# A fused attention and expert kernel: key weights folded like the query weights, in 16 tiles turned by DMA, and a new order of the first loads

## The chip, the core and the metric

The kernel runs on one core of a Trainium2 chip. A core has five engines with a queue each: PE (matrix products; its weight loads are listed as PEld), DVE and ACT (elementwise work and copies), POOL (elementwise work) and SP (here it only issues transfers, as ACT does for some). The transfers of all queues run on 16 DMA engines. The metric is the time of one execution in microseconds (us); lower is better.

## The reference, cut to what matters

There are 2048 tokens of width 1024, 32 heads of width 32, all in bf16.

```python
qkv = x @ wqkv                                     # [2048, 3 x 1024]: q, k, v
pq = q . w_phi ; pk = k . w_phi                    # per head, w_phi is 32 x 32
phi_q = concat(softmax(pq), softmax(-pq))          # 64 features a head; phi_k likewise
kv = phi_k^T v ; z = sum(phi_k)
a = ((phi_q kv) / (phi_q z + 1e-6)) @ wo           # linear attention
i = argmax(x @ w_r)                                # one token is chosen
y = (silu(x_i @ w_gate) * (x_i @ w_up)) @ w_down   # an expert of width 3584 for that token
b = x, with y * sigmoid(r_i) added to row i
g = sigmoid(x . gate_w)
out = g * a + (1 - g) * b
```

## The kernel before, in words

Tokens are worked on in 16 tiles of 128 (index `t`); the inner dimension 1024 is cut in 8 blocks of 128 (`kb`). Since `x @ w @ w_phi` is `x @ (w w_phi)`, the kernel first folds `w_phi` into the key and query weights: `wkf` and `wqf`, 128 x 8 x 1024 each. All products then need the transposed tokens `xT`.

Its stages follow each other on PE:

- *Start.* `spin` runs matmuls on constants while the first loads are under way. Token tiles 0 and 1 are transposed on PE (`xT_tile`, line 285), all others by DMA (`xT_dma`, line 299). `v_first` (line 595) computes the values of tiles 0 and 1, block by block as `wv_sb` arrives in eight loads (line 277). Two small rows (`rows`) are turned by one matmul (`rows_in`) into two more columns of `wv_sb`; they give the router and gate products.
- *Value stage.* `k_v(t, c)` computes the values of one tile in three column parts (`c` = 0, 1, 2, of 256, 384 and 386 columns), eight matmuls each, and ACT copies them out. Between these parts the weights are folded. The transposed weight blocks come by DMA (`wT_load`, line 304) into the buffers `shv`, eight blocks for keys, then eight for queries in the same places.
- *Key stage.* `feats(u, wkf, False)` for 32 units of half a tile (eight matmuls of 512 columns and the softmax), then `k_kv` (`kvps`).
- *Query stage.* `feats(u, wqf, True)`, a DMA turn, `q_num` (`num`) and the output product `q_wo` (`po`), interleaved by due times in a running count of PE time.
- *Expert.* Its three rounds and a half of gate and up weights (`gu_load`, `ffn_gu`, `facc`) run at units 9, 16 and 23 of the key stage, the down product in the query stage. The weight chunks (`wch`) go through buffers that other things have left: W and V (one tile), A (a ring of three), D (the two `shv`), X and Y (the place of `wv_sb`).

The folds of keys and queries differ. For a key block, `fold` multiplies by a block-diagonal 128 x 128 matrix `BDm` with four copies of `w_phi` a block: eight matmuls of 128 columns, two casts on DVE, and the result stands in `wkf` as it is used. For the queries, `qfold` works in 32 x 32 tiles of PE, 16 at a time:

```python
nc.tensor.matmul(banks[r][32*c:32*c+32, :]..., lhsT=BDm[32*r:32*r+32, j, 32*r:32*r+32],
                 rhs=shv[half][32*r:32*r+32, :, j*P:(j+1)*P], ..., tile_position=(32*r, 32*c))
```

Four such packs (table `PACKS`) give the transposed folded weight `wfT`, in two buffers of the ring that A uses too; eight DMA transposes (`qfold_turn`, line 334) turn it into `wqf` during the key stage, after units 4 and 7. `q_heads` (line 161) reads the turned weight in its head order.

Where nothing pins an instruction, the scheduler of the language may move it on its queue; `tc.keep_in_program_order` pins it. Each transfer of SP and ACT has one of eight completion semaphores in turn, so it waits for the one issued eight before it. `gate_load` (line 459) lets POOL write one element of the first three weight chunks after the last `wT_load` has landed, which keeps the expert's loads behind the transposes. `route` finds the chosen token after the last values; `route_row` loads its row.

Of the kernel before, what the change touches and what calls it, by code (L numbers as in the profile page):

```python
# [38 lines left out]
FOLDS = [0] * 5 + [1] * 8 + [0] * 3  # L39
PACKS = {(13, 2): (0, 0), (14, 1): (1, 0), (15, 0): (0, 1), (15, 2): (1, 1)}  # L40
# [3 lines left out]
def general_path(tc, A_wqkv, A_w_phi, A_wo, x2, out2, gate, omg, y2, idx_pool, xT, wqf, ident, BDm):  # L44
# [27 lines left out]
    oo = gp.tile([P, D], BF, name="g_oo")  # L72

    nc.sync.dma_start(out=wv[:], in_=w_v[:, :, 2 * D:3 * D])
# [95 lines left out]
def kernel(  # L170
# [8 lines left out]
    wphi_v = A_w_phi.rearrange("(j hq) d f -> hq d j f", hq=4)  # L179
# [21 lines left out]
    def spin(n):  # L201
        for _ in range(n):
            nc.tensor.matmul(small_ps[:, 0:512], lhsT=ones, rhs=ones4, start=True, stop=True)
# [5 lines left out]
    BDm = const.tile([P, KB, P], BF, name="BDm")  # L209
    ones4 = nc.const_aps.tensor_like(1.0, BDm[:, 0:4, :].rearrange("p j f -> p (j f)"))  # L210
    rows = const.tile([P, P], BF, name="rows")
    nc.vector.memset(rows[:], 0.0)
    nc.vector.memset(BDm[:], 0.0)
    xT = big.tile([P, KB, S], BF, name="xT")
    wqf = big.tile([P, KB, D], BF, name="wqf")
# [50 lines left out]
    def xload(t, eng):  # L266
        xt_ = shv[1][:, 2 + t, :]
        eng.dma_start(out=xt_, in_=x2[t * P:(t + 1) * P, :])
        xtiles[t] = xt_
# [3 lines left out]
    xload(1, nc.scalar)  # L273
    nc.scalar.dma_start(out=rows[0:KB, :], in_=B_w_r.rearrange("(kb p) -> kb p", p=P))
    nc.scalar.dma_start(out=rows[KB:2 * KB, :], in_=gate_w.rearrange("(kb p) -> kb p", p=P))
    for kb in range(KB):
        nc.sync.dma_start(out=wv_sb[:, kb, 0:D], in_=w_v[:, kb, 2 * D:3 * D])  # L277

    def rows_in():
        rows_ps = m2_ps[:, 0:2 * KB]  # L280
        nc.tensor.matmul(rows_ps, lhsT=rows[:], rhs=ident[:, 0:2 * KB], start=True, stop=True)
        nc.vector.tensor_copy(out=wv_sb[:, :, D:VW].rearrange("p k c -> p c k"),
                              in_=rows_ps.rearrange("p (c k) -> p c k", c=2))

    def xT_tile(t):
        xt_ = xtiles.pop(t)
        for q4 in range(4):
            pool, tag = ((psB, "pB"), (psA, "pA"))[q4 // 2]
            pT = pool.tile([P, 2, P], F32, name="pT", tag=tag)
            for k2 in range(2):  # L290
                kb = q4 * 2 + k2
                nc.tensor.matmul(pT[:, k2, :], lhsT=xt_[:, kb * P:(kb + 1) * P], rhs=ident[:], start=True, stop=True)
            (nc.vector.tensor_copy if q4 % 2 == 0 else nc.scalar.copy)(
                out=xT[:, q4 * 2:q4 * 2 + 2, t * P:(t + 1) * P], in_=pT[:])
            if (t, q4) == (1, 3):
                nc.vector.tensor_copy(out=m2_ps[0:1, 0:1], in_=xT[0:1, 5, P:P + 1])
                rows_in()

    def xT_dma(t):
        nc.sync.dma_start_transpose(out=xT[:, :, t * P:(t + 1) * P], in_=x2[t * P:(t + 1) * P, :])  # L300
# [3 lines left out]
    def wT_load(which, kb):  # L304
        n = kb
        wT[which, kb] = shv[n // 4][:, n % 4, :].rearrange("p (k f) -> p k f", f=P)
        nc.sync.dma_start_transpose(out=wT[which, kb],
                                    in_=A_wqkv[kb * P:(kb + 1) * P, (1 - which) * D:(2 - which) * D])

    def fold(which, wf, kb):  # L310
        for jh in range(2):
            pW = psB.tile([P, 4, P], F32, name="pW", tag="pB")
            for j4 in range(4):
                j = jh * 4 + j4
                nc.tensor.matmul(pW[:, j4, :], lhsT=wT[which, kb][:, j, :], rhs=BDm[:, j, :],  # L315
                                 start=True, stop=True)
            nc.vector.tensor_copy(out=wf[:, kb, jh * 512:(jh + 1) * 512].rearrange("p (j f) -> p j f", f=P), in_=pW[:])  # L317

    def qfold(a, half):
        if (a, half) == (0, 0):  # L320
            moe["wfT"] = [ring.tile([P, 4, D], BF, name="wfT", tag="wch") for _ in range(2)]
        pB = psB.tile([P, 512], F32, name="pW", tag="pB")
        banks = [b[:] for b in vbank + [pB]]
        for r in range(4):
            for c in range(4):
                j = 4 * a + c
                nc.tensor.matmul(banks[r][32 * c:32 * c + 32, :].rearrange("p (k d) -> p k d", d=P),  # L327
                                 lhsT=BDm[32 * r:32 * r + 32, j, 32 * r:32 * r + 32],
# [467 lines left out]
    while i < 2 * NU or n_next < NU or wos:  # L796
# [50 lines left out]
        if i == 0:  # L847
            route_row()
# [89 lines left out]
```

## Time and profile before

| | us |
|---|---|
| median of three runs (lowest, highest) | 267.17 (266.39, 267.59) |
| the profiled execution | 266.67 |
| its span | 265.0 |
| PE busy | 258.0 |
| DVE busy | 181.9 |
| POOL busy | 126.3 |
| ACT busy | 124.8 |

The span is measured on the engines and lies 1.67 us under the time of the same execution. Busy times of matmuls overlap, so what a matmul costs is read from the starts of those that follow each other, not from its duration. The rows below come from the page of this execution and from queries of its trace.

### The profile page before, as it was taken

To read this page: it belongs to the slowest core of one execution; us is meant where nothing else is said; L and a number is where in the kernel's file an instruction comes from. 1 tells how busy PE (TensorE), PEld (TensorE's weight loads), DVE (VectorE), ACT (ScalarE), POOL (GpSimd) and SP (SyncE) were. 2 spreads that over 40 slices of the span, in tenths; PEclk is the share of its full clock that TensorE was granted. 3 is DMA by queue.
4 is the path that set the end of the run, shared out by engine and by line. 5 is a ranking of instruction groups with operands and counts; after the bars stand their busy time and mean duration, and the time that the engine had idled before them with its cause. 6 is when DMAs were issued, how large, how long until landed. Compare 5 with 4: busy or idle time off the path is not lost.

```text
span 265.0 us, 5298 instructions
## 1 busy us (share of the span) xinstructions
PE 258.0 (97%) x1976; PEld 138.8 (52%) x1999; DVE 181.9 (69%) x319; ACT 124.8 (47%) x257; POOL 126.3 (48%) x86
## 2 busy tenths in 40 slices
PE   7999999999999999999999999999999999999994
PEld 2666767765444554545555455455444544544542
DVE  4010323315789685998788789799898797898872
ACT  3143333337776454554556676447362553435210
POOL 6000000000084999579989887655536555455001
PEclk9999999999999999999999999999999999999998
DMA  7989999938999869999958999998999899979742
GB/s 228 255 143 200 187 170 189 151 79 310 405 359 201 189 102 391 401 356 362 383 200 322 208 172 182 181 215 200 242 210 197 155 195 158 227 150 179 182 119 68
DMA packets 110970, 58.45 MB, mean 221 GB/s; under 512 B 93580, under 2 KB 98780, under 8 KB 110940
## 3 DMA queue, kind: packets, MB, share of 16 engines
q1 hardware_dynamic: 108140, 53.39, 84.1%
q10 hardware_dynamic: 2768, 4.67, 7.2%
q8 instruction: 17, 0.28, 0.5%
q14 instruction: 13, 0.11, 0.1%
q0 software_dynamic: 32, 0.00, 0.0%
HBM read 31.27 MB, written 4.20 MB: 134 GB/s over the span
## 4 chain that ended last, share of the span: by engine, by line
PE 95%; DMA 2%; issue 1%; SPq 0%; DVE 0%; ACT 0%
PE pq L622 21%; PE pk L622 21%; PE po L726 21%; PE pv L583 19%; PE kvps L653 3%; PE num L687 3%; PE facc L519 2%; DMA wv_sb<-in_A_wqkv_dram 2%; PE pW L315 1%; PE pv L609 1%; PE small_ps L537 1%; PE vbank L609 1%; PE vbank L327 1%; DVE oo L730 0%; SPq L277 0%
## 5 line engine op out<-in xcount | busy, mean ns | idle before, releaser
L640 POOL TENSOR_TENSOR phi<-e,rq 128x1024 bf16<-128x1024 bf16 x63 | 119.6, 1912 | 65.3 <-DVE rq L636 38.8
L632 DVE TENSOR_REDUCE ssum<-e 128x32 f32<-128x1024 bf16 x64 | 77.4, 1211 | 16.2 <-ACT e L628 16.1
L622 PEld LDWEIGHTS <-xT 128*128 128x128 bf16 x512 | 47.4, 98 | 52.3 <-issue 1.1
L622 PE MATMUL pq<-wqf,xT 128*128 128x512 bf16 x256 | 60.3, 379 | 0.0
L622 PE MATMUL pk<-wkf,xT 128*128 128x512 bf16 x245 | 59.2, 379 | 0.6
L726 PE MATMUL po<-wo_sb,oT 128*128 128x512 bf16 (+2 forms) x252 | 58.4, 372 | 0.6
L583 PE MATMUL pv<-wv_sb,xT 128*128 128x256 bf16 (+2 forms) x336 | 50.8, 307 | 0.0
L583 PEld LDWEIGHTS <-xT 128*128 128x128 bf16 x336 | 31.9, 97 | 15.4 <-issue 0.5
L591 ACT CAST v_all<-pv 128x384 bf16<-128x384 f32 (+1 forms) x45 | 20.1, 448 | 36.8 <-PE pv L583 31.1
L726 PEld LDWEIGHTS <-oT 128*128 128x128 bf16 x264 | 23.9, 98 | 23.3
L627 ACT ACTIVATE e<-pq 128x512 bf16<-128x512 f32 x32 | 18.9, 592 | 36.2 <-PE pq L622 34.5
L317 DVE CAST wkf<-pW 128x512 bf16<-128x512 f32 x16 | 10.3, 686 | 32.1 <-PE pW L315 32.1
L627 ACT ACTIVATE e<-pk 128x512 bf16<-128x512 f32 x32 | 19.1, 597 | 27.9 <-PE pk L622 23.4
L730 DVE SCALAR_TENSOR_TENSOR oo<-po,gate,xg 128x512 bf16<-128x512 f32 (+2 forms) x33 | 24.0, 727 | 4.4 <-PE po L726 4.3
L461 POOL COPY wch<-shv 1x1 bf16<-1x1 bf16 x3 | 0.4, 177 | 54.0 <-DMA shv<-in_A_wqkv_dram 54.0
L636 DVE RECIPROCAL rq<-ssum 128x32 f32<-128x32 f32 x64 | 21.8, 342 | 1.3
L692 DVE TENSOR_TENSOR o_sb<-num,rden 128x512 bf16<-128x512 f32 x32 | 21.6, 674 | 0.8
L628 ACT ACTIVATE e<-pk 128x512 bf16<-128x512 f32 x32 | 18.9, 591 | 0.0
L628 ACT ACTIVATE e<-pq 128x512 bf16<-128x512 f32 x32 | 18.9, 590 | 0.0
L711 ACT ACTIVATE xg<-xin,omg 128x1024 f32<-128x1024 bf16 x16 | 18.4, 1149 | 0.4
L687 PEld LDWEIGHTS <-phT 128*128 128x128 bf16 x256 | 12.4, 98 | 7.8 <-issue 0.3
L653 PEld LDWEIGHTS <-phi 128*128 128x128 bf16 x256 | 11.8, 98 | 7.6 <-issue 0.8
(129 smaller groups left out, 149.9 us busy)
## 6 DMA issues: line engine op xcount, KB each, us to landing
wch<-in_B_w_down_dram SPq DMA_DIRECT2D x7, 1024.0 KB
wch<-in_B_w_up_dram SPq DMA_DIRECT2D x6, 1024.0 KB
wch<-in_B_w_gate_dram SPq DMA_DIRECT2D x4, 1024.0 KB
xin<-in_A_x_dram ACTq DMA_DIRECT2D x16, 256.0 KB
out_dram<-oo SPq DMA_DIRECT2D x30, 128.0 KB
wch<-in_B_w_gate_dram SPq DMA_DIRECT2D x4, 768.0 KB
wv_sb<-in_A_wqkv_dram SPq DMA_DIRECT2D x8, 256.0 KB
wo_sb<-in_A_wo_dram SPq DMA_DIRECT2D x1, 2048.0 KB
```

Of the source, the lines that this page charges most:

```text
L583: nc.tensor.matmul(pv[:, 0:hi - lo], lhsT=xT[:, kb, t * P:(t + 1) * P], rhs=wv_sb[:, kb, lo:hi], start=(kb == 0), stop=(kb == KB - 1))
L591: copy(out=v_all[:, t, h0:h1, 0:DH], in_=pv[:, 0:(h1 - h0) * DH].rearrange("p (h d) -> p h d", d=DH))
L622: nc.tensor.matmul(pk[:].rearrange("p (c r) f -> p c r f", r=4) if is_q else pkf, lhsT=xT[:, kb, t * P:(t + 1) * P], rhs=q_heads(wf, kb, h ...
L627: nc.scalar.activation(out=e[:, :, 0, :], in_=pk[:], func=ACTF.Exp)
L628: nc.scalar.activation(out=e[:, :, 1, :], in_=pk[:], func=ACTF.Exp, scale=-1.0)
L632: nc.vector.tensor_reduce(out=ssum[:], in_=e2, axis=AX.X, op=ALU.add)
L636: nc.vector.reciprocal(out=rs, in_=ssum[:])
L640: eng.tensor_tensor(out=phi[:].rearrange("p h s f -> p (h s) f"), in0=e2, in1=_bc(rs, [P, HH * 2, DH]), op=ALU.mult)
L687: nc.tensor.matmul(num[:, pl * 66:pl * 66 + 66], lhsT=phT[:, pl, :], rhs=KV[hf][:, pl, :], start=True, stop=True)
L692: nc.vector.tensor_tensor(out=st["o"][:, hf * HH:(hf + 1) * HH, :].rearrange("p (r h) d -> p r h d", h=2), in0=nv[:, :, :, 0:DH], in1=rden ...
L726: nc.tensor.matmul(po[:, 0:w], lhsT=st["oT"][:, kb, :], rhs=moe["wo"][:, kb, sl], start=(kb == 0), stop=(kb == KB - 1))
L730: nc.vector.scalar_tensor_tensor(out=o_out[:, 0:w], in0=po[:, 0:w], scalar=gate[:, t:t + 1], in1=st["xg"][:, sl], op0=ALU.mult, op1=ALU.add)
```

## The change

Three things are changed.

- The key weights are folded as the query weights are: four more packs of 16 matmuls, after parts (5, 1), (6, 0), (8, 2) and (9, 1) of the value stage, in place of eight times eight matmuls with `BDm`. The results stand in the place of `wqf`, which is free until the query turns, and eight DMA transposes turn them into `wkf`. `BDm` is now built on the rarely taken general path alone; `w_phi` comes in one load (`wph`) where four filled `BDm`. The key features read `wkf` through `q_heads`.
- Token tile 1 is loaded by SP behind tile 0, where ACT loaded it. Both tiles are transposed on PE before the first value product, one constant matmul fewer stands ahead, and `v_first` takes its parts in another order.
- The order of SP's queue is pinned: key turns 0 to 3, the last four query blocks, key turns 4 to 7, and behind them the first expert chunks. The gate on POOL is gone. The first two chunks of the third round go ahead of the second four query turns. The last value parts of tiles 14 and 15 come in another order (`ORDER`), and `route` is called when three of them are still to come, where before one was.

```diff
-FOLDS = [0] * 5 + [1] * 8 + [0] * 3
-PACKS = {(13, 2): (0, 0), (14, 1): (1, 0), (15, 0): (0, 1), (15, 2): (1, 1)}
+PACKS = {(5, 1): (0, 0, 0), (6, 0): (0, 1, 0), (8, 2): (0, 0, 1), (9, 1): (0, 1, 1),
+         (13, 2): (1, 0, 0), (14, 1): (1, 1, 0), (15, 0): (1, 0, 1), (15, 2): (1, 1, 1)}
+ORDER = {14: ((14, 2), (15, 2), (14, 0)), 15: ((14, 1), (15, 0), (15, 1))}
...
 xload(0, nc.sync)
-xload(1, nc.scalar)
...
 for kb in range(KB):
-    nc.sync.dma_start(out=wv_sb[:, kb, 0:D], in_=w_v[:, kb, 2 * D:3 * D])
+    if kb == 0:
+        xload(1, nc.sync)
+    pin(nc.sync.dma_start(out=wv_sb[:, kb, 0:D], in_=w_v[:, kb, 2 * D:3 * D]))
...
-    def fold(which, wf, kb):
-        for jh in range(2):
-            pW = psB.tile([P, 4, P], F32, name="pW", tag="pB")
-            for j4 in range(4):
-                j = jh * 4 + j4
-                nc.tensor.matmul(pW[:, j4, :], lhsT=wT[which, kb][:, j, :], rhs=BDm[:, j, :],
-                                 start=True, stop=True)
-            nc.vector.tensor_copy(out=wf[:, kb, jh * 512:(jh + 1) * 512]..., in_=pW[:])
-    def qfold(a, half):
+    def fold(which, a, half):
         if (a, half) == (0, 0):
-            moe["wfT"] = [ring.tile([P, 4, D], BF, name="wfT", tag="wch") for _ in range(2)]
+            if which == 0:
+                wfT[0] = [wqf[:, 4 * n:4 * n + 4, :] for n in range(2)]
+            else:
+                wfT[1] = [ring.tile([P, 4, D], BF, name="wfT", tag="wch")[:] for _ in range(2)]
...
-                                 lhsT=BDm[32 * r:32 * r + 32, j, 32 * r:32 * r + 32],
+                                 lhsT=wph[32 * r:32 * r + 32, j, :],
...
-    def qfold_turn(ar):
-        nc.sync.dma_start_transpose(out=wqf[:, :, ar * P:(ar + 1) * P], in_=moe["wfT"][ar // 4][:, ar % 4, :])
+    def fold_turn(which, ar):
+        return nc.sync.dma_start_transpose(out=(wkf, wqf)[which][:, :, ar * P:(ar + 1) * P],
+                                           in_=wfT[which][ar // 4][:, ar % 4, :])
...
     def gu_load(r, kp, where):
         w = wbuf(where)
-        gate_load(w[0:1, 0:1])
...
     def v_first():
+        spin(6)
+        xT_tile(0)
+        xT_tile(1)
...
+        part(0, 0, 0)
+        part(0, 0, 1)
+        rows_in()
+        for t, kb, c in ((1, 0, 0), (0, 1, 0), (0, 1, 1), (1, 0, 1), (1, 1, 0), (1, 1, 1),
+                         (0, 0, 2), (1, 0, 2), (0, 1, 2), (1, 1, 2)):
+            part(t, kb, c)
+        for kb in range(2, KB - 1):
+            for t in range(2):
+                for c in range(3):
+                    part(t, kb, c)
...
-                             rhs=q_heads(wf, kb, hf) if is_q else wf[:, kb, hf * 512:(hf + 1) * 512],
+                             rhs=q_heads(wf, kb, hf),
...
+            if (t, n) in PACKS:
+                fold(*PACKS[t, n])
+            if (t, n) == (8, 2):
+                for ar in range(4):
+                    pin(fold_turn(0, ar))
+            if (t, n) == (9, 1):
+                for kb in range(4, KB):
+                    wT_load(1, kb)
+                for ar in range(4, 8):
+                    pin(fold_turn(0, ar))
+                moe["gu", 0] = [gu_load(0, k, b) for k, b in enumerate("WV")]
...
         if i in (QT0, QT1):
+            if i == QT1:
+                moe["gu", 1] += [gu_load(1, 2, "Y"), gu_load(1, 3, "A")]
+                moe["gu", 2] = [gu_load(2, k, b) for k, b in enumerate("WV")]
             for a in range(h, h + 4):
-                qfold_turn(a)
+                pin(fold_turn(1, a))
```

At the start, PE before has the transposes of tile 1 (`pT`) between value products (`vbank` is tile 0, `pv` tile 1); the rows begin with the last transpose that stands ahead of the first product.

```order
L292 MATMUL pT<-ident,shv 128x128
L609 LDWEIGHTS xT
L609 MATMUL vbank<-wv_sb,xT 128x256
L292 LDWEIGHTS shv
L292 MATMUL pT<-ident,shv 128x128
L292 LDWEIGHTS shv
L292 MATMUL pT<-ident,shv 128x128
L609 LDWEIGHTS xT
L609 MATMUL vbank<-wv_sb,xT 128x384
```

Now, from the same place:

```order
L301 MATMUL pT<-ident,shv 128x128
L605 LDWEIGHTS xT
L605 MATMUL vbank<-wv_sb,xT 128x256
L605 LDWEIGHTS xT
L605 MATMUL vbank<-wv_sb,xT 128x384
L290 LDWEIGHTS rows
L290 MATMUL small_ps<-ident,rows 128x16
L605 LDWEIGHTS xT
L605 MATMUL pv_199<-wv_sb,xT 128x256
L605 LDWEIGHTS xT
L605 MATMUL vbank<-wv_sb,xT 128x256
```

All 16 transposes now stand ahead of the first product; three products of block 0 follow, and the next one needs block 1.

On SP's queue, the end of the value stage before (`xT` are token tiles, `shv` weight blocks, `wch` expert chunks, `mrow` the router's result):

```order
L300 DMA_TRANSPOSE xT<-in_A_x_dram 128x8x128 x4
L307 DMA_TRANSPOSE shv<-in_A_wqkv_dram 128x8x128 x8
L495 DMA wch<-in_B_w_gate_dram 128x2x2048 x4
L369 DMA mrow<-mi 1x16x2
L495 DMA wch<-in_B_w_gate_dram 128x2x1536
```

Now, from the last token tile on:

```order
L308 DMA_TRANSPOSE xT<-in_A_x_dram 128x8x128
L341 DMA_TRANSPOSE wkf<-wqf 128x8x128 x4
L315 DMA_TRANSPOSE shv<-in_A_wqkv_dram 128x8x128 x4
L341 DMA_TRANSPOSE wkf<-wqf 128x8x128 x4
L495 DMA wch<-in_B_w_gate_dram 128x2x2048 x2
L376 DMA mrow<-mi 1x16x2
```

The eight key turns (`wkf<-wqf`) are new; the last four of them stand behind every other transpose of the stage and ahead of the expert's first chunks.

SP's queue around the query turns (`wqf<-wfT`) of the key stage, before:

```order
L335 DMA_TRANSPOSE wqf<-wfT 128x8x128 x4
L495 DMA wch<-in_B_w_gate_dram 128x2x1536
L335 DMA_TRANSPOSE wqf<-wfT 128x8x128 x4
L528 DMA gT<-gs 4x1x128 x4
L495 DMA wch<-in_B_w_up_dram 128x2x512
L495 DMA wch<-in_B_w_up_dram 128x2x2048 x4
```

Now:

```order
L341 DMA_TRANSPOSE wqf<-wfT 128x8x128 x4
L495 DMA wch<-in_B_w_gate_dram 128x2x1536
L495 DMA wch<-in_B_w_up_dram 128x2x512
L495 DMA wch<-in_B_w_gate_dram 128x2x1536
L495 DMA wch<-in_B_w_up_dram 128x2x512
L495 DMA wch<-in_B_w_up_dram 128x2x2048 x2
L341 DMA_TRANSPOSE wqf<-wfT 128x8x128 x4
L533 DMA gT<-gs 4x1x128 x4
```

The two chunks of 128x2x2048 of the third round, which wait for the first round's products to have left W and V, now stand ahead of the second four query turns.

## Rows read from the trace of the kernel before

**Rows 1.** The page: span, busy time, granted clock and DMA share in slices, chain.

```profile
span 265.0 us, 5298 instructions
...
PE 258.0 (97%) x1976; PEld 138.8 (52%) x1999; DVE 181.9 (69%) x319; ACT 124.8 (47%) x257; POOL 126.3 (48%) x86
...
PEclk9999999999999999999999999999999999999998
DMA  7989999938999869999958999998999899979742
...
PE 95%; DMA 2%; issue 1%; SPq 0%; DVE 0%; ACT 0%
```

**Rows 2.** PE's waits: engine, line, what it waited for; us in total, times, longest.

```profile
PE vbank L609 <- DMA wv_sb<-in_A_wqkv_dram: 0.6, 1, 0.6
```

**Rows 3.** The chain that ended last: start us, us, what.

```profile
1.79 4.85 DMA wv_sb<-in_A_wqkv_dram
...
27.81 0.45 PE pW L315 x8
28.25 3.48 PE pv L583 x24
...
59.22 0.35 PE vbank L327 x12
59.59 2.28 PE pv L583 x16
...
68.05 0.32 PE pk L622
...
79.03 1.73 PE pk L622 x8
```

**Rows 4.** Groups by line and shape: busy us, mean ns of one | idle before.

```profile
L622 PE MATMUL pq<-wqf,xT 128*128 128x512 bf16 x256 | 60.3, 379 | 0.0
L622 PE MATMUL pk<-wkf,xT 128*128 128x512 bf16 x245 | 59.2, 379 | 0.6
```

**Rows 5.** Timeline of the start, PE: start us, us, what [idle before].

```profile
0.91 3.15 PE L203 MATMUL small_ps<-const-bfloat16-1.0 128*128 128x512 bf16 x7 [0.91 <-PEq L922]
...
4.21 0.62 PE L292 MATMUL pT<-ident,shv 128*128 128x128 bf16 x8
...
6.67 0.27 PE L609 MATMUL vbank<-wv_sb,xT 128*128 128x256 bf16 x1 [0.61 <-DMA wv_sb<-in_A_wqkv_dram]
...
8.16 0.27 PE L609 MATMUL vbank<-wv_sb,xT 128*128 128x256 bf16 x1
...
12.52 0.27 PE L609 MATMUL vbank<-wv_sb,xT 128*128 128x256 bf16 x1
...
13.73 14.08 PE L583 MATMUL pv<-wv_sb,xT 128*128 128x256 bf16 x96
```

**Rows 6.** Timeline of SP's queue in the value stage (merged rows give their count).

```profile
7.66 2.98 SPq L300 DMA_TRANSPOSE xT<-in_A_x_dram  x1
...
10.77 1.98 SPq L759 DMA_DIRECT2D BDm<-in_A_w_phi_dram  x4
12.79 1.24 SPq L300 DMA_TRANSPOSE xT<-in_A_x_dram  x1
...
22.99 1.31 SPq L307 DMA_TRANSPOSE shv<-in_A_wqkv_dram  x1
...
48.58 4.50 SPq L307 DMA_TRANSPOSE shv<-in_A_wqkv_dram  x2
...
55.77 1.23 SPq L307 DMA_TRANSPOSE shv<-in_A_wqkv_dram  x1
```

**Rows 7.** Timeline of POOL: the gate copies of the first chunks.

```profile
59.27 0.41 POOL L461 COPY wch<-shv 1x1 bf16<-1x1 bf16 x3 [53.98 <-DMA shv<-in_A_wqkv_dram]
```

**Rows 8.** Timeline of SP's queue: the query turns.

```profile
79.17 5.71 SPq L335 DMA_TRANSPOSE wqf<-wfT  x4
...
87.35 7.78 SPq L335 DMA_TRANSPOSE wqf<-wfT  x4
```

More of the change, by code (lines that the diff above doesn't have):

```diff
@@ L72, in general_path @@
     oo = gp.tile([P, D], BF, name="g_oo")
+    BDm = gp.tile([P, KB, P], BF, name="g_BDm")
+    nc.vector.memset(BDm[:], 0.0)
+    for hq in range(4):
+        sl = slice(hq * 32, (hq + 1) * 32)
+        nc.vector.tensor_copy(out=BDm[sl, :, sl], in_=wph[sl, :, :])
     nc.sync.dma_start(out=wv[:], in_=w_v[:, :, 2 * D:3 * D])
@@ L199, with spin @@
     kpool = kscope.enter_context(tc.tile_pool(name="kpool", bufs=1))
-    def spin(n):
+    pin = tc.keep_in_program_order
+    def spin(n, bank=None):
         for _ in range(n):
-            nc.tensor.matmul(small_ps[:, 0:512], lhsT=ones, rhs=ones4, start=True, stop=True)
+            pin(nc.tensor.matmul((small_ps if bank is None else bank)[:, 0:512], lhsT=ones, rhs=ones4,
+                                 start=True, stop=True))
     ident = const.tile([P, P], BF, name="ident")
@@ L738, in q_store @@
             eng.dma_start(out=dst, in_=src)
-    wq = [(0, kb) for kb in range(KB)] + [(1, kb) for kb in range(KB)]
-    fq = list(wq)
-    wn = {"want": 0, "done": 0, "folded": 0}
-    def wload(n):
-        wn["want"] += n
-        while wq and wn["done"] < min(wn["want"], wn["folded"] + 8):
-            wT_load(*wq.pop(0))
-            wn["done"] += 1
-    spin(7)
-    xT_tile(0)
-    xT_tile(1)
     v_first()
@@ L757 @@
     with nc.allow_non_contiguous_dma(reason="tiny loads"):
-        for hq in range(4):
-            nc.sync.dma_start(out=BDm[hq * 32:(hq + 1) * 32, :, hq * 32:(hq + 1) * 32], in_=wphi_v[hq])
+        pin(nc.sync.dma_start(out=wph[:], in_=wphi_v))
     for t in range(TX):
         xT_dma(TX + t)
-        wload(1)
-    for t in range(2, TX):
-        for c in range(3):
-            k_v(t, c)
-    for t in range(TX, NT):
-        if t + TX < NT:
-            xT_dma(t + TX)
-            wload(1)
-        for n, c in enumerate((2, 0, 1) if t == NT - 1 else (0, 1, 2)):
-            k_v(t, c)
-            if n == 1 and t == NT - 1:
-                route()
-            if n >= 3 - FOLDS[t]:
-                w, kb = fq.pop(0)
-                fold(w, wkf if w == 0 else wqf, kb)
-                wn["folded"] += 1
-                wload(4 if t + TX >= NT else 0)
-            if (t, n) in PACKS:
-                qfold(*PACKS[t, n])
+        wT_load(0, t)
+    for t in range(2, NT):
+        if t >= 4 and t < 8:
+            xT_dma(t + TX)
+            wT_load(0, t)
+        if t == 8:
+            for n in range(4):
+                wT_load(1, n)
+                xT_dma(12 + n)
+        for n, (tc_, c) in enumerate(ORDER.get(t, ((t, 0), (t, 1), (t, 2)))):
+            k_v(tc_, c)
+            if (t, n) == (NT - 2, 2):
+                route()
+            if (t, n) in PACKS:
+                fold(*PACKS[t, n])
[8 more added lines that the diff above has]
+                moe["gu", 0] = [gu_load(0, k, b) for k, b in enumerate("WV")]
     vscope.close()
@@ L848 @@
             route_row()
+            moe["gu", 1].append(gu_load(1, 1, "X"))
         if i == 7:
@@ L905 @@
     with tc.If(moe["fv"] > 0):
-        general_path(tc, A_wqkv, A_w_phi, A_wo, x2, out2, gate, omg, moe["y2c"][:, 1, :], ip, xT, wqf, ident, BDm)
+        general_path(tc, A_wqkv, A_w_phi, A_wo, x2, out2, gate, omg, moe["y2c"][:, 1, :], ip, xT, wqf, ident, wph)
     keep.close()
```

89 lines of the change are left out of this document (43 added, 46 removed).

## The prediction

> **What bounds the kernel now.** I read the page first. PE is busy for 258.0 us of a span of 265.0, and 95% of the chain that ended last is PE [rows 1]. Then PE's waits: after the start there is one on a transfer, 0.6 us [rows 2]. So from the first value products on, the time is the sum of what PE issues, and the question at each place is whether PE has less to issue and whether a transfer then becomes late. The chain in order of time gives the price of each piece, as the distance between starts [rows 3]. The timeline of the start shows the one place where PE waits for loads [rows 5], and SP's queue shows the second resource that could bind: the value stage is filled with DMA transposes at 9 tenths of DMA share, with a gap at the end of the stage, slice 9, where the share is 3 tenths [rows 1, 6]. The change takes work off PE and puts eight more transposes on that queue.
>
> **The folds.** Before, eight key folds of eight matmuls each stand on the chain. The first begins at 27.81 and the value product behind it at 28.25: 0.44 to 0.45 us each, together 3.56 us [rows 3]. After, four more packs take their place. A pack begins at 59.22 and the next product at 59.59 [rows 3], 0.37 us; with 0.36 us for the other three, whose rows read alike, four cost 1.46 us. PE saves 2.10 us. The key features read the turned weight in the query features' order; those have the same mean for one matmul, 379 ns against 379 ns [rows 4], so this costs nothing. The copies of a pack are two on DVE and two on ACT. The query packs of before have the same ones, two value parts apart, and PE waited for none of them [rows 2], so I take 0; if each of the four new packs had to wait as long as it takes, 0.37 us, it would be 1.5 us and the time that of the clock's rival below.
>
> **The start.** Before, block 0 of the value weights is there in time, but block 1 takes from 1.79 for 4.85 us [rows 3], and PE, idle for 0.61 us, goes on at 6.67 [rows 5]. From then on nothing waits. One block of six products takes 0.872 us: five blocks lie between 8.16 and 12.52 [rows 5]. The value stage proper begins at 13.73. Eight blocks would take 6.98 us, so 13.73 - 6.67 = 7.06 us show that almost all of it is done after block 1 has come. After, three products of block 0 (two of 256 columns, one of 384, about 0.38 us by their share of 2052 columns in 0.872 us) and all 16 transposes stand ahead of the first product on block 1. If block 1 lands as before, the rest takes 6.98 - 0.38 = 6.60 us and the stage begins at 13.27: 0.46 us saved. The landing is what I don't know. Its issue comes one issue later, some 0.45 us, since tile 1 now goes ahead of it on SP; against that, the bytes that must arrive ahead of it are the same, since tile 1 came through ACT's queue before. Bounds: 0.45 us later or, with tile 1 no longer moved beside it, 0.6 us earlier (no wait at all). That is a saving between 0 and 1.06 us. I take 0.46, the nearest row.
>
> What decides between these is whether loads of two queues share the engines. The Trainium skill, "DMA: Bandwidth & Descriptors", section "Queues, rings and completion order", says that a DMA engine takes turns between the queues it has work for, packet by packet. By that rule tile 1 took its share from tile 0 and block 0 before, block 1 has the same bytes ahead of it either way, and the sum stays as it is; only tile 0 would land sooner. No row here shows the order of packets.
>
> **The first pack.** It needs the first four key blocks. The fourth of them was issued from 22.99 to 24.30 [rows 6]. A transpose lands about 2.3 us after its issue ends: the last one ended at 57.00 and POOL, which waited for it, went on at 59.27 [rows 6, 7]. So it landed at about 26.5. After, the four `BDm` loads of 1.98 us [rows 6] are one load; the transposes come between 0 and 1.5 us sooner, so it lands between 25.0 and 26.5. PE reaches the pack at 13.27 + three tiles of 3.48 + two parts (640 of 1026 columns, 2.17) = 25.9. A stall lies between 0 and 0.6 us; I take 0.
>
> **The key turns.** From token tile 4 to the last key turn SP now issues 36 transposes. Before, 25 steps lie between the starts 12.79 and 48.58: 1.43 us each, stalls included [rows 6]. Starting at 11.8 (between 11.3 and 12.8 by the saved loads), they end at 11.8 + 36 x 1.43 = 63.3 and the last lands at 65.6. Turns that read on-chip memory took 5.71 / 4 = 1.43 in one row and 7.78 / 4 = 1.95 in the other, beside expert loads [rows 8]; here they have none beside them, and I take 1.43. The key stage would begin at 68.05 - 2.10 - 0.46 = 65.5. Its first unit reads the half that the first four turns wrote, which land about 54; the second unit, one unit of 1.73 us [rows 3] later, at 67.2, reads the other half. The cover is 1.6 us. The last four query blocks are issued ahead of the second four turns, 5.7 us sooner, and land at about 59.9; the pack that needs them stands two value parts and two packs (2.9 us) before the key stage, at 62.6: nothing.
>
> **The rest.** The expert's first chunks leave SP at about 63, where POOL let them go at 59.27 before [rows 7]; they are used at unit 9 of the key stage, so nine units of 1.73 us [rows 3] or more, 15 us, cover them. Routing comes sooner. The third round's two chunks wait on SP until the first round has run; behind them stand the second query turns, which are needed only for the query stage, over 20 such units or 35 us later, and four small transfers for the expert. PE hides all of it, and nothing late in the kernel becomes later than now. Taking the POOL gate away frees nothing that was waited for. I take 0.
>
> **Sum.** 266.67 (the profiled execution: 265.0 of span and 1.67 around it) - 2.10 - 0.46 = 264.1. The median of the runs is 267.17, 0.5 above that execution; a median of the changed kernel would be 267.17 - 2.56 = 264.6.
>
> **Rivals.**
> First, the key turns land late and the second key unit waits. For it speaks that SP's queue has only 1.6 us of cover, against it the 1.43 us of 25 steps. If all eight turns cost the 1.95 us of the slower row, they land 8 x 0.52 = 4.2 us later, the stall is 2.6 us, and the time is 267.2: no change. That is the point from which it decides: any dearer turn makes the kernel slower. The dearest transpose of these rows, 2.98 us beside the first value loads [rows 6], would make it 12.4 us late, a stall of 10.8 and a time of 275.4. The other side ends there.
> Second, PE's clock. The seven constant matmuls of 512 columns take 3.15 us, which is 1.2 GHz, and the eight transposes of 128 columns right behind them 0.62 us, which is 2.4 GHz [rows 5]: the clock rose after PE had been busy without a break from 0.91. (The line of the granted clock, which reads 9 tenths or more in the first slice too [rows 1], doesn't show it; the distances do.) Now one constant matmul is missing, and PE pauses before and after the transposes. If the clock rises only when PE has run as long again from block 1 on, 3.15 us at half rate do half the work: 1.6 us lost, 266.2. Against it: the pause of before, 0.61 us at 6.05, did not lower the clock. The Trainium skill, "TensorE: Matmul & The Clock Gate", section "Part 1: The HAM clock gate", says that the slow level is the default and that activity lifts it; by that rule the pause that the missing matmul leaves speaks for this rival.
> Third, block 1 comes 0.45 us later and the first pack waits 0.6: only 1.5 us remain, 265.7.
> Fourth, the start gains all that it can, 1.06 us: 264.0.
>
> **How the numbers follow.** The forecast (264.1 to 265.2, most of the bounds of the start) has 0.66, the fourth rival 0.06, the third 0.08, the clock 0.07, late turns up to no change 0.07, late turns beyond it 0.06. A measurement of this kernel tells about 0.5%, 1.3 us, from no change; faster by more than that (under 265.8) holds the forecast, the fourth, the third and 0.01 of the late turns, 0.81; within it lie the clock and 0.06 of the late turns, 0.13; slower is the rest, 0.06. I predict 264.5, a tenth under the sum for the fourth. The range reaches from 263.4, the fourth rival and the spread of the runs below it (0.6 us), to 266.3, which takes in the third rival and the clock.
>
> **What would show it.** Right: matmuls of 128 columns with `wkf` gone and 64 more of 32 rows; value products of the stage proper from about 13.3; the first key unit at about 65.5 and everything behind it shifted by the same 2.6 us, with no wait of PE over 0.5 us after 7 us. Wrong: a wait of PE on a transfer `wkf<-wqf` at the second key unit, a wait on `shv` at the first pack (about 26), or value products spaced at 1.2 GHz after 7 us. If block 1 lands at a quite different time than 6.6, the term of the start is wrong by that much.

## The result: slower, 271.23 us

The changed kernel took 271.23 us, median of four runs (269.45 to 271.85), against 267.05 us for the kernel before on the same chip (266.39 to 267.59). The ratio is 1.0147, 95% interval 1.012 to 1.0174. I had forecast 264.5 us and given a slower kernel 0.06: the prediction was wrong in its sign. The profiled execution took 271.03 us, 4.36 above that of before.

The page of the changed kernel, which answers to [rows 1]: span, busy time, granted clock and DMA share in 40 slices, shares of the chain.

```profile
span 269.4 us, 5309 instructions
...
PE 259.0 (96%) x1986; PEld 136.2 (51%) x1998; DVE 176.3 (65%) x309; ACT 128.7 (48%) x265; POOL 126.1 (47%) x83
...
PEclk9999999999999999997999999999999999999999
DMA  6999999999999999899959998997999896979642
...
PE 85%; DMA 10%; DVE 1%; SPq 1%; issue 1%; ACT 0%; DVEq 0%
```

Of the chain, 10% are now transfers, where it was 2%, and the granted clock has a dip in the nineteenth slice, 121 to 128 us. PE's waits say which transfers (answers to [rows 2]; us in total, times, longest):

```profile
PE facc L522 <- DMA wch<-in_B_w_up_dram: 2.7, 2, 2.1
...
PE small_ps L398 <- DMA rows<-in_A_x_dram: 1.2, 1, 1.2
...
PE vbank L605 <- DMA wv_sb<-in_A_wqkv_dram: 0.2, 1, 0.2
```

PE's timeline gives the balance by stage (start us, us, what; the idle time before a row in brackets). These rows answer to [rows 3, 5].

```profile
13.42 12.77 PE L588 MATMUL pv<-wv_sb,xT 128*128 128x256 bf16 x88
...
65.99 8.81 PE L636 MATMUL pk<-wkf,xT 128*128 128x512 bf16 x40
...
81.89 0.18 PE L398 MATMUL small_ps<-ident,rows 128*128 128x8 bf16 x1 [1.16 <-DMA rows<-in_A_x_dram]
...
118.14 0.61 PE L522 MATMUL facc<-wch,xs 128*32 128x512 bf16 x8 [0.57 <-DMA wch<-in_B_w_up_dram]
120.85 0.70 PE L522 MATMUL facc<-wch,xs 128*32 128x512 bf16 x8 [2.10 <-DMA wch<-in_B_w_up_dram]
...
121.91 3.25 PE L636 MATMUL pk<-wkf,xT 128*128 128x512 bf16 x8
...
141.59 1.89 PE L636 MATMUL pq<-wqf,xT 128*128 128x512 bf16 x8
```

The value stage proper begins 0.31 us sooner than before (13.42 against 13.73) and takes 52.57 us instead of 54.25: the key stage begins 1.99 us sooner. Then the gain is lost. From the first key product to the first query product it took 67.98 to 137.61 before, 69.63 us; now 65.99 to 141.59, 75.60. These 5.97 us hold three waits: 1.16 us for the row of the chosen token, 0.57 and 2.10 us for the two chunks of the fourth expert round (its 16 matmuls stand right behind the 32 of the third). And behind the last wait PE ran slowly: a key unit of eight products took 3.06 us there instead of 1.73, the eight expert products 0.70 and the eight of `kvps` 0.56 (rows of the chain, below), together some 1.9 us more. The query stage and the end add about 0.4.

### The profile page after: what moved, and what is told of

The parts are those of the page before. It is cut to its first block, busy times and chain, and to the rows that moved or that the text cites. A ratio compares the mean times of both kernels' runs of the same rounds, so it can differ in the third digit from the quotient of the medians.

```text
span 269.4 us, 5309 instructions
## 1 busy us (share of the span) xinstructions
PE 259.0 (96%) x1986; PEld 136.2 (51%) x1998; DVE 176.3 (65%) x309; ACT 128.7 (48%) x265; POOL 126.1 (47%) x83
## 4 chain that ended last, share of the span: by engine, by line
PE 85%; DMA 10%; DVE 1%; SPq 1%; issue 1%; ACT 0%; DVEq 0%
PE pq L636 21%; PE po L740 20%; PE pv L588 18%; PE pk L636 14%; DMA wch<-in_B_w_up_dram 4%; PE num L701 3%; PE kvps L667 3%; DMA mrow<-mi 3%; DMA rows<-in_A_x_dram 2%; DMA wv_sb<-in_A_wqkv_dram 2%; PE facc L522 2%; PE vbank L605 1%; PE pv L605 1%; PE small_ps L542 1%; DVE ssum L646 1%; PE vbank L331 1%
## 5 line engine op out<-in xcount | busy, mean ns | idle before, releaser
L654 POOL TENSOR_TENSOR phi<-e,rq 128x1024 bf16<-128x1024 bf16 x63 | 119.8, 1912 | 123.5 <-ACT e L642 65.8
L636 PE MATMUL pk<-wkf,xT 128*128 128x512 bf16 x256 | 61.1, 385 | 0.0
L588 PE MATMUL pv<-wv_sb,xT 128*128 128x256 bf16 (+2 forms) x336 | 50.2, 307 | 0.0
L337 DVE CAST wqf<-vbank 128x512 bf16<-128x512 f32 x8 | 5.2, 686 | 23.3 <-PE pW L331 23.3
L337 DVE CAST wfT<-vbank 128x512 bf16<-128x512 f32 x8 | 5.2, 682 | 17.2 <-PE pW L331 17.2
```

What stands on the lines that cost most here:

```text
L588: nc.tensor.matmul(pv[:, 0:hi - lo], lhsT=xT[:, kb, t * P:(t + 1) * P], rhs=wv_sb[:, kb, lo:hi], start=(kb == 0), stop=(kb == KB - 1))
L636: nc.tensor.matmul(pk[:].rearrange("p (c r) f -> p c r f", r=4), lhsT=xT[:, kb, t * P:(t + 1) * P], rhs=q_heads(wf, kb, hf), start=(kb == ...
L654: eng.tensor_tensor(out=phi[:].rearrange("p h s f -> p (h s) f"), in0=e2, in1=_bc(rs, [P, HH * 2, DH]), op=ALU.mult)
```

## Where the transfers became late

SP's queue in the changed kernel (start us, us, what, count); the first row is the second set of key turns, the rows of `wqf` are the query turns, which answer to [rows 8]:

```profile
58.40 5.92 SPq L341 DMA_TRANSPOSE wkf<-wqf  x4
64.37 1.11 SPq L495 DMA_DIRECT2D wch<-in_B_w_gate_dram  x2
...
88.55 1.69 SPq L495 DMA_DIRECT2D wch<-in_B_w_up_dram  x3
90.36 14.02 SPq L341 DMA_TRANSPOSE wqf<-wfT  x4
104.48 3.13 SPq L533 DMA_DIRECT2D gT<-gs  x4
107.65 0.45 SPq L495 DMA_DIRECT2D wch<-in_B_w_up_dram  x1
...
108.89 1.47 SPq L495 DMA_DIRECT2D wch<-in_B_w_up_dram  x3
```

In the kernel before, the first chunks left SP at 59.47:

```profile
59.47 3.31 SPq L495 DMA_DIRECT2D wch<-in_B_w_gate_dram  x4
```

Now they leave at 64.37, and the second four query turns hold SP until 104.38, not 95.13 [rows 8]. What that does to the DMA engines stands in the busy times by stretch. Columns: stretch, its length, then busy time (and number of instructions) of PE, PEld, DVE, ACT and POOL, granted clock, DMA share, GB/s. First two stretches of the kernel before, then five of the changed one.

```profile
62.00:66.00 4.00, 4.00 (x55) 2.29 (x40) 1.96 (x4) 2.90 (x9) 0.00 (x0) 1.00 1.03 418
...
86.00:90.00 4.00, 3.95 (x41) 1.97 (x35) 2.03 (x5) 1.71 (x4) 4.00 (x3) 1.00 0.56 132
```

```profile
62.00:66.00 4.00, 4.00 (x56) 2.15 (x55) 2.83 (x13) 2.40 (x7) 0.00 (x0) 1.00 0.93 179
...
98.00:102.00 4.00, 4.00 (x54) 1.79 (x52) 3.19 (x5) 2.39 (x5) 3.92 (x3) 1.00 1.21 201
...
106.00:110.00 4.00, 4.00 (x36) 2.10 (x33) 3.83 (x9) 2.42 (x6) 1.91 (x1) 1.00 0.40 80
110.00:114.00 4.00, 4.00 (x35) 2.07 (x32) 3.96 (x8) 2.18 (x5) 3.51 (x2) 1.00 1.03 416
...
122.00:126.00 4.00, 4.00 (x23) 1.70 (x21) 0.15 (x1) 0.92 (x3) 1.71 (x1) 0.67 1.06 385
```

Read the last two columns. Chunk loads alone fill the engines at 386 to 420 GB/s (62 to 78 and 102 to 118 in the kernel before). Turns fill them too (share 1.21), with half the bytes, 201 GB/s. So while turns run, few chunks come. The kernel before had room in between: a share of 0.56 in 86 to 90 and of 0.50 in 94 to 98. And in 106 to 110 the engines stood mostly idle: SP had just come out of the turns and was issuing small tables (`gT`), and the next chunks were behind those. These were the last four gate and up chunks, of 1 MB each, and PE needed the last of them for the fourth round; at 400 GB/s I estimate 10.5 us for the four. The chain shows the last one, which landed at 120.8, and what PE did behind it. It also shows the row's two transfers, which took 7.02 and 4.61 us for 0.1 and 2 KB while chunks were moving:

```profile
65.58 7.02 DMA mrow<-mi
...
77.24 4.61 DMA rows<-in_A_x_dram
...
109.88 10.93 DMA wch<-in_B_w_up_dram
...
120.85 0.70 PE facc L522 x8
121.55 0.56 PE kvps L667 x8
122.10 3.06 PE pk L636 x8
```

## The experiments

Two theories stood at the start: the order at the second query turns is the loss; or the key turns are, since they push every later transfer back. The table has what all twelve runs showed. "Stage" is the key stage from first `pk` to first `pq` (69.63 in the kernel before), "waits" are PE's in it, for the row and for the fourth round's chunks (other waits are named in the text).

| kernel | value stage from | key stage from | stage, us | row, us | chunks, us | ratio to before, 95% |
|---|---|---|---|---|---|---|
| changed | 13.42 | 65.99 | 75.60 | 1.16 | 2.67 | 1.0147 (1.012 to 1.0174) |
| s1 start alone | 14.96 | 69.22 | 69.63 | 0 | 0 | 1.0001 (0.9976 to 1.0027) |
| e1 turns first | 13.11 | 65.68 | 72.14 | 0.82 | 0.66 | 1.0009 (0.9983 to 1.0034) |
| e3 four key turns less | 14.81 | 67.37 | 70.06 | 0 | 0.25 | 0.9957 (0.9934 to 0.998) |
| g1 both of these | 13.22 | 66.10 | 69.63 | 0 | 0 | 0.9955 (0.9921 to 0.9989) |
| e4 router row first | 13.22 | 65.78 | 75.62 | 0.75 | 3.23 | 1.0165 (1.0106 to 1.0223) |
| e14 = e1 and e4 | 14.87 | 67.43 | 71.23 | 0.65 | 0.60 | 1.0014 (0.999 to 1.0038) |
| k1 = e14, row by POOL | 13.76 | 66.33 | 72.28 | 1.32 | 0.73 | 1.006 (1.004 to 1.008) |
| k2 = k1, third round later | 15.19 | 67.75 | 71.55 | 0.90 | 0 | 1.0232 (1.0204 to 1.0261) |
| k3 = k2, more spins | 13.64 | 66.22 | 71.61 | 0.97 | 0 | 1.0243 (1.0217 to 1.0269) |
| f6 last chunks earlier | 13.23 | 66.56 | 75.17 | 0.77 | 3.12 | 1.0103 (1.0061 to 1.0145) |
| f3 = e1, last chunks earlier | 14.67 | 67.23 | 70.56 | 0 | 0.75 | 1.0022 (1.0003 to 1.004) |
| f5 = f3, row later on PE | 13.19 | 66.51 | 72.44 | 0 | 0.53 | 1.0051 (1.0022 to 1.0079) |

In the five rows whose value stage begins at 14.67 or later, PE's clock rose late in the profiled execution (see the start, below): PE comes everywhere some 1.4 us later there, and its waits are shorter by up to that.

**Turns first (e1).** The third round's first two chunks go behind the second query turns; all else as changed.

```diff
             if i == QT1:
                 moe["gu", 1] += [gu_load(1, 2, "Y"), gu_load(1, 3, "A")]
-            if i == QT1:
-                moe["gu", 2] = [gu_load(2, k, b) for k, b in enumerate("WV")]
             for a in range(h, h + 4):
                 pin(fold_turn(1, a))
+            if i == QT1:
+                moe["gu", 2] = [gu_load(2, k, b) for k, b in enumerate("WV")]
```

> Only the order at the second query turns is put back: the two chunks of the third round (W, V) stand behind the four turns, all else as in the changed kernel. Theory A (the wait of 2.7 us at the last expert matmuls comes from that order: 4 MB of chunks stand ahead of the turns, so SP sits 14 us in pushing them and issues the last four chunks only from 107.65 on): turns pushed by about 99, last chunks issued by about 105, wait at the last expert matmuls under 0.5 us, PE clock stays high, so 2.7 + about 1.9 us come back: about 266.5 us, with the wait of 1.2 us on the token row still there. Theory B (the chunks as a whole start 5 us later because eight key turns hold SP until 64.3, and order only shifts the wait): the wait stays above 1.5 us, 269 to 271 us.

Measured: 267.19 us. The turns, the chunks' wait and the stretch that had been idle:

```profile
89.17 9.60 SPq L341 DMA_TRANSPOSE wqf<-wfT  x4
```

```profile
118.69 0.62 PE L522 MATMUL facc<-wch,xs 128*32 128x512 bf16 x8 [0.66 <-DMA wch<-in_B_w_up_dram]
```

```profile
106.00:110.00 4.00, 4.00 (x37) 2.11 (x34) 3.83 (x9) 2.42 (x6) 1.91 (x1) 1.00 1.02 402
```

The turns take 9.60 instead of 14.02, the idle stretch is full of chunks, the wait falls from 2.67 to 0.66, and PE's clock stays up. That is 4 us by one pair of loads, as theory A had it, though the wait stays above its 0.5 and the time above its 266.5. The kernel is no faster than before: its key stage begins 2.3 us sooner and is 2.5 us longer. PE waits for the row (0.82), for POOL's features (0.51) and for a chunk. And the room that the kernel before had is gone: from 62 to 118 no stretch of 4 us has a DMA share under 0.87, and 86 to 90 reads

```profile
86.00:90.00 4.00, 4.00 (x37) 2.11 (x36) 2.21 (x3) 1.67 (x3) 4.00 (x3) 1.00 0.95 206
```

**Four key turns less (e3).** Half of the key features' weights are set to zero, not turned; the order at the query turns stays as changed.

```diff
-                for ar in range(4, 8):
-                    pin(fold_turn(0, ar))
+                nc.gpsimd.memset(wkf[:, :, 4 * P:8 * P], 0.0)
```

> The last four key turns are left out (half of the folded key weights is set to zero instead, so that part of the result is not computed); all else as in the changed kernel, the order at the second query turns too. Theory B (late start of the chunks): first chunks leave SP at about 58.5 in place of 64.4, the wait at the last expert matmuls is gone, and the wait on the token row too, 265 to 266 us. Theory A alone (the order at the query turns decides, since the third round's chunks wait there for the first round's products whatever came before): the wait at the last expert matmuls stays above 1.5 us, 268 to 270 us.

Measured: 266.23 us. The chunks leave SP at 58.84, and with that the row's wait is gone and the chunk's is 0.25, although the order of the loads is still the changed one. So the order alone is not the cause. PE's rows at the third and fourth rounds:

```profile
115.71 2.34 PE L522 MATMUL facc<-wch,xs 128*32 128x512 bf16 x40
118.30 0.62 PE L522 MATMUL facc<-wch,xs 128*32 128x512 bf16 x8 [0.25 <-DMA wch<-in_B_w_up_dram]
```

PE came to the third round when it does in the changed kernel (115.66), so the shorter wait is the chunk's: it was used from 118.30, not from 120.85. For the row the profile doesn't decide, since PE came to it 1.2 us later (81.96 against 80.73, late clock).

**Both (g1).** What remains of e1's loss is the question here: the edits of e1 and e3 together.

> The kernel with the second query turns put back ahead of the third round's chunks, and besides without the last four key turns (the second half of the turned key weights is set to zero by GpSimd instead, so half the key features are left out). In the kernel with the order put back the key stage, from its first product to the query stage's, took 72.14 us, against 69.63 in the kernel before; its DMA engines were busy (share 0.87 or more) in every 4 us from 62 to 118. Theory E (what the folds save is lost again because the key turns hold SP and the DMA engines till 65, so the expert chunks start 5 us later than before and the stretch up to the fourth round is bound by them): without four turns the chunks start at 59 again, no wait for the token row or for a chunk is above 0.3 us, the key stage takes 69.7 to 70.2, and the time falls 1.5 to 2.3 us below the 267.2 of the order alone: 264.9 to 265.7. Rival (the waits have to do with the routing chain on VectorE and GpSimd, or the stretch is bound by other loads): the row's wait of 0.8 and the chunk's of 0.7 stay and the time stays at 267.

Measured: 265.33 us. Chunks on SP's queue, then PE: the third and fourth rounds run as one row of 48, and the key stage takes 69.63.

```profile
58.81 1.09 SPq L495 DMA_DIRECT2D wch<-in_B_w_gate_dram  x2
```

```profile
66.10 8.81 PE L636 MATMUL pk<-wkf,xT 128*128 128x512 bf16 x40
...
114.44 2.77 PE L522 MATMUL facc<-wch,xs 128*32 128x512 bf16 x48
...
135.73 1.89 PE L636 MATMUL pq<-wqf,xT 128*128 128x512 bf16 x8
```

This is what I expected of the key turns' share: with SP and the DMA engines free of four turns at 58.8, PE's saving ahead of the key stage (66.10 against 67.98, 1.88 us) arrives at the query stage whole (135.73 against 137.61). The kernel leaves work out, so it is a measure of the turns, not a version to use. It takes away the turns' time on SP and their load on the DMA engines at once; no run parts the two.

**The router's row, and who issues it (e4, e14, k1).** Could the row be early if its small transfers were not behind chunks? In e4 and e14 the router's row goes ahead of the first chunks; in k1 the chosen row is also issued by POOL, past SP's queue.

```diff
-                moe["gu", 0] = [gu_load(0, k, b) for k, b in enumerate("WV")]
+    moe["gu", 0] = [gu_load(0, k, b) for k, b in enumerate("WV")]
     vscope.close()
...
-        idx_sp = nc.values_load(ixi[0:1, 0:1], engines=[ET.SP], min_val=0, max_val=S - 1)
-        nc.sync.dma_start(out=rows[0:KB, :], ...
+        idx_sp = nc.values_load(ixi[0:1, 0:1], engines=[ET.Pool], min_val=0, max_val=S - 1)
+        nc.gpsimd.dma_start(out=rows[0:KB, :], ...
```

> The first two chunks are issued behind the router's small transfer (mrow) in place of ahead of it, all else as in the changed kernel. If the 1.2 us wait on the token row comes from mrow standing behind 2 MB of chunks (7.0 us to land), mrow lands in about 2 to 3 us, the index is there about 2 us sooner, that wait is gone and the rest is as in the changed kernel: its 2.7 us wait at the last expert matmuls stays or grows by up to 1 us, 269.5 to 271 us. If the token row is late because it stands itself behind the chunks (4.6 us to land), the wait stays above 0.8 us and the time at 271.

> Both: second query turns ahead of the third round's chunks, and the router's small transfer ahead of the first chunks. If both waits have the causes named, neither is left, the clock stays high and what the folds (1.7 us measured in the value stage) and the start (0.3 us) gave remains: about 265 us. If theory B holds, 268 us or more.

> As the kernel with both orders put back (second query turns ahead of the third round's chunks, router's small transfer ahead of the first chunks), and the chosen token's row is loaded on POOL's queue in place of SP's. Theory C: the row lands near 82 us in every version so far because it stands on SP's queue behind 5 MB of chunks, whenever it is issued; that leaves the kernel before under 0.7 us of slack there, and a PE that is 2 us ahead must wait. By C the wait of 0.65 us on the row is gone and the first round of the expert begins about 1 us sooner; the last expert matmuls then wait about 1.5 us, so the time stays near 267. Rival D: the row is late because its index is late (router, DVE and the load of a register), not for its transfer: then the wait stays within 0.3 us of what it was.

Measured: 270.94, 267.35 and 268.44 us. None took the wait away; e14, forecast at 265, and k1, which was to free the row, missed. In k1 POOL began the issue at 76.45 and the row landed 6.2 us later, in a stretch with a DMA share of 1.02 to 1.04; the wait was 1.32. So SP's order alone is not what keeps the row; that it is what the transfer meets on the DMA engines fits, but no run took the chunks away to show it. The Trainium skill, "DMA: Bandwidth & Descriptors", section "Issuing engines are not separate DMA queues", says that SP, ACT and POOL all feed the same 16 DMA engines; k1 agrees (6.2 us from POOL, 4.61 from SP in the changed kernel).

**The third round later (k2, k3).** Should the chunks be given more time instead? k2 puts the third round two key units later; k3 adds four constant matmuls at the start.

```diff
-    GU = (9, 16, 23)
+    GU = (9, 16, 25)
...
+        spin(3)
         xT_tile(1)
+        spin(1)
```

> As the one with the row on POOL's queue, and the third round of the expert runs at unit 25 of the key stage in place of 23 (4 us later). If nothing but these waits stood between the saving on PE and the end, PE waits for no transfer after the start, and the value stage's 1.7 us and the start's 0.3 to 0.6 us show in full: 264.5 to 265.3 us in a run whose clock rises early, about 1.4 us more in one where it rises late. If the saving is lost in another way (POOL or DVE becoming late in the key stage), 266.5 or more.

> As the one with the third round later, with four more constant matmuls on PE at the start: three between the transposes of token tiles 0 and 1, one behind them. Theory E: in some runs of the new start PE stays at 1.2 GHz until about 9.4 us and the value stage proper begins 1.4 us later (14.8 in place of 13.1 to 13.4 in two of five profiles), because the missing constant matmul and the pauses around the transposes leave PE less busy. By E the clock is high by 6 us in this profile, and the median is 0.3 to 0.8 us under the one without them. Rival: when the clock rises is chance and not changed by them; then the median is the same or up to 0.5 us more for the time they take.

Measured: 272.99 and 273.56 us, the slowest. The chunks' wait is gone and stands elsewhere, in the query stage (k2, PE's timeline, then SP's queue):

```profile
159.47 0.43 PE L701 MATMUL num<-KV,phT 128*128 128x66 bf16 x8 [2.98 <-DMA phT<-phi]
```

```profile
109.41 14.05 SPq L479 DMA_DIRECT2D wch<-in_B_w_down_dram  x2
...
147.53 0.57 SPq L479 DMA_DIRECT2D wch<-in_B_w_down_dram  x1
```

SP stands 14 us at two down-weight loads, till 123.5: by the code they take buffers that the moved round reads, and that ran at 122. A later use frees a buffer later. The last down load then leaves at 147.53, behind the first turn of the query features, where in k1 all seven were gone by 136.5; the turn issued at 148.20 landed 11.22 us later, and that is PE's wait. In k1 the turn issued at 149.39 took 8.45. That the late load makes the difference is likely, not shown. Nor did k3's matmuls help: its profile has the early clock, but its median is 0.57 above k2's.

**Issue times of the last chunks (f6, f3), and the row later on PE (f5).** f6 keeps the changed order, f3 and f5 have the turns first; f5 also moves the row's transpose on PE from unit 7 to unit 8 of the code. Its expectation calls that two key units; in the traces it is one (nine units stand ahead of it in f5, eight in f3).

```diff
...
         if i == 13:
-            moe["gu", 2].append(gu_load(2, 2, "A"))
+            moe["gu", 2] += [gu_load(2, 2, "A"), gu_load(2, 3, "D")]
+            moe["gu", 3] = [gu_load(3, 0, "A")]
...
-        if i == 7:
+        if i == 8:
             xs_turn()
```

> The changed kernel with its order at the second query turns kept (two chunks of the third round ahead of them), but with the third round's fourth chunk and the fourth round's first issued right behind its third chunk, so that SP no longer issues the 16-row table of the round before (0.58 us, and its wait for ScalarE) ahead of them. Theory A (the order at the turns is the loss: the turns hold SP till 104.4 whatever comes after them, and the last chunks are late by that): the fourth chunk leaves SP about 1 us earlier (107.9 instead of 108.9), the wait of 2.10 us falls to about 1.1, the first wait of 0.57 stays, the token row's wait of 1.16 stays, and the time is 269 to 271. Theory D (what is late is only what stands behind the table, the turns do no harm): the waits of the third round go and PE's clock stays up there: 267 to 268.

> Both: the order at the second query turns put back (turns first), and the third round's fourth chunk and the fourth round's first issued right behind its third chunk. With turns first alone, the third round still waited 0.66 us and the token row 0.82 us. Theory A: the 0.66 goes, the row's wait of about 0.8 stays: 266.3 to 267.0. Theory that the DMA engines are full in that stretch and issue times don't decide: the wait of 0.6 stays or moves to another chunk: 267.2.

> As the kernel with the turns first and the last chunks earlier, and PE's transpose of the chosen token's row stands two key units later in its order (16 key products and 16 accumulations further on), the first expert round 2.6 units later. If PE's wait for the row (0.82 to 1.16 us) is a loss of its own, it goes and the time falls by about 0.8 more: 265.5 to 266.2. If the later first round only hands the wait on (its buffers come free 5 us later, so the second round's chunks are issued later and land late), a wait of 1 us or more appears at the second or third round: 267 or more.

Measured: 270.66, 267.25 and 268.16 us. f6's time is in theory A's range, but its waits of 0.93 and 2.19 are not (0.57 and 1.1). Two of its rows show why: SP is out of the turns no sooner and issues the tables first, so the burst of chunks still begins at 109, and little moves in the stretch ahead of it (36 GB/s).

```profile
109.28 1.47 SPq L495 DMA_DIRECT2D wch<-in_B_w_up_dram  x3
```

```profile
106.00:110.00 4.00, 4.00 (x34) 2.07 (x32) 3.50 (x6) 2.42 (x6) 2.12 (x2) 1.00 0.72 36
```

In f3 three chunks are issued sooner, and the wait of 0.75 stays: there the engines run at 386 to 412 GB/s from 102 to 118, and the last of four rounds' bytes comes when it comes. That was the second theory of f3. In f5 the row's wait is gone, but PE then waits 1.40 us for POOL's features and 0.53 for a chunk. Here a wait that was taken away came back elsewhere.

**The start alone (s1).** The kernel before with only the new start: tile 1 ahead of block 1 on SP, transposes and first products in the new order, one constant matmul less.

```diff
-    xload(1, nc.scalar)
...
     for kb in range(KB):
-        nc.sync.dma_start(out=wv_sb[:, kb, 0:D], in_=w_v[:, kb, 2 * D:3 * D])
+        if kb == 0:
+            xload(1, nc.sync)
+        pin(nc.sync.dma_start(out=wv_sb[:, kb, 0:D], in_=w_v[:, kb, 2 * D:3 * D]))
...
```

> The kernel before with the change of the start alone (both token tiles first on SP's queue, all transposes ahead of the products, one constant matmul fewer, the new order of products); folds, turns and the expert as before. If the start's saving of 0.3 to 0.6 us holds and the clock rises early: 266.6 us, and no wait on the token row above 0.2 us. If the clock rises late as in two of five profiles of the new start: the value stage proper begins near 15, and the time is 267.5 to 268.3.

Measured: 267.15 us, ratio 1.0001, with an interval of about 0.7 us to either side. No gain shows, one of 0.3 us isn't ruled out, and its profile shows a case of my second rival (below).

## Why the prediction was wrong

**The step that failed is "The rest"**: "nine units of 1.73 us [rows 3] or more, 15 us, cover them", "PE hides all of it, and nothing late in the kernel becomes later than now", and, at its end, "I take 0". I gave each transfer its own cover and found each wide. But the chunks of four rounds, the turns and the row share 16 engines, and in the kernel before these are full from 62 to 78 and from 102 to 118, with some room in between. I had the row for it: the slices of [rows 1] behind the gap, most of them at 9. What had to be covered was the sum of what the engines carry, not each load. Eight key turns push the first chunks from 59.47 to 64.37: five microseconds, by my estimate 2 MB at 400 GB/s, that the stretch has to make up. Beside that, the moved pair of chunks makes the second query turns wait on SP and leaves an idle stretch when they are done. And behind those turns stood not only the four small transfers that I listed but the last four gate and up chunks, whose wait costs most. In key stages that began at 65.7 to 66.1, the order costs 3.46 us (75.60 to 72.14) and four key turns a further 2.51 (72.14 to 69.63); by the medians it is 4.0 and 1.9. The two don't add: with four turns gone the order makes no difference that the ratios show (0.9957 and 0.9955), with all eight there it makes 1.0147 of 1.0009. That key turns and order together are the loss is shown, since g1's key stage takes the 69.63 of the kernel before. That in e1 it is the full engines which bind, and not SP, is argued from the shares and from f3.

I also wrote that "Routing comes sooner". It did on PE; the row landed at 81.85, and PE came to it at 80.73. In the kernel before it had come later and found the row there:

```profile
82.57 0.17 PE L391 MATMUL small_ps<-ident,rows 128*128 128x8 bf16 x1
```


**The key turns themselves: right.** They end at 64.3 (expected 63.3), and PE waited at neither key unit. My first rival, which had this wait, didn't come; its place, SP's queue, was right, its victim was not the key features but the expert.

**The folds: right in kind, 0.4 too large.** The value stage shrank by 1.68 us, not 2.10. A pack takes 0.37 us as read, but the products behind it also take longer:

```profile
26.56 2.29 PE pv L588 x16
```

Sixteen products of a part take 2.17 by the share of their columns in 3.48; behind a pack 2.28 to 2.29, which [rows 3] show too (59.59). A pack costs 0.48: 52.57 less 14 tiles of 3.48 is 3.85, over eight packs. I read the pack's own row and not the one behind it.

**The start: 0.31 us in the profile (0.46 forecast, within its bounds), nothing that the runs of s1 can tell.** PE's rows there, and the granted clock of a stretch:

```profile
8.21 0.53 PE L600 MATMUL vbank<-wv_sb,xT 128*128 128x386 bf16 x1
...
14.96 1.36 PE L583 MATMUL pv<-wv_sb,xT 128*128 128x256 bf16 x10
```

```profile
6.00:8.00 2.00, 2.00 (x12) 1.24 (x10) 0.65 (x2) 0.61 (x2) 0.00 (x0) 1.00 0.97 319
```

A product of 386 columns takes 0.53 us here and 0.33 in the changed kernel's profile; only from 9.5 do the rows run at 2.4 GHz, and the stage proper begins at 14.96. This is what the second rival priced at 1.6 us; it came at 1.54 (14.96 against 13.42), but not in every execution. Of 13 profiles with the new start (k3's with four matmuls more) it stands in five (s1, e3, e14, k2, f3), eight begin at 13.1 to 13.8. What decides it is not shown. Whether the old start has such executions stays open: I have one profile of it.

**The first pack** waited for nothing in the changed kernel's profile, as taken; in f5 and f6 it waited 0.7, just above the 0.6 that I gave as its most.

Not settled: 0.24 us of the key stage's 5.97, the 0.4 behind it, and 0.5 of e1's 2.51 that no listed wait holds. No version that computes everything beat the kernel before; g1 suggests where to look: a way to turn the key weights that leaves the DMA engines to the first chunks.

## What to carry to other kernels

Where a change puts transfers on a queue, add up what all DMA engines must carry until the last use in that stretch, at the rate that the windows show; a load's own distance to its use proves nothing when the engines are full. An order of loads and turns is judged by whether the engines ever stand idle behind it. And a short wait can cost twice, once as itself and once as slow matmuls behind it: some 1.9 us in the changed kernel, nothing in f6.

## Hardware behaviour not expected

Two waits of PE of 0.57 and 2.10 us with eight short matmuls (0.61 us) between them were followed by eight matmuls in 3.06 us instead of 1.73 and a granted clock of 0.67 in that stretch, a mix of the two levels, 1.2 and 2.4 GHz. In e4 the same happened (0.82 and 0.75 in 118 to 126). But in f6 waits of 0.93 and 2.19 us with the same eight matmuls between were followed by a key unit at full rate, and the granted clock stayed at 1.00:

```profile
122.60 0.62 PE L522 MATMUL facc<-wch,xs 128*32 128x512 bf16 x8 [2.19 <-DMA wch<-in_B_w_up_dram]
...
123.41 1.89 PE L636 MATMUL pk<-wkf,xT 128*128 128x512 bf16 x8
```

The changed kernel's row there is 121.91 3.25. So how long PE waited does not by itself tell whether its clock falls. A single wait of 0.66 (e1) was followed by no fall, a single one of 2.98 (k2) by eight matmuls in 2.93 us. In s1 the granted clock reads 1.00 from 6 to 8 us while matmuls run at half rate. Transfers of 2 KB or less took 4.6 to 7.0 us beside chunk loads.
